# Dilated convolution with gated output on one core: order of the first and the last steps, and padded tiles at the end

## The chip, the core and the metric

The kernel runs on one core of one Trainium2 chip. The metric is the time of one launch in microseconds (us) on the device. A lower time is better. A core has five engines with instruction streams of their own: TensorE (PE in the profile, with its weight loads as PEld), VectorE (DVE), ScalarE (ACT), GpSimd (POOL) and SyncE (SP). DMA transfers are issued by SP, ACT and POOL and run beside the engines.

## The reference

The input x has two sequences of 16000 tokens with 144 channels. A causal convolution with 15 taps, two tokens apart, makes 288 channels. The first 144 go through tanh, the other 144 through a sigmoid, their product z goes through a 144 by 144 matrix. All arrays are bf16.

```python
B, T, D, K = (2, 16000, 144, 15)
def reference(x, w, w_o):
    dil = 2
    pad = (K - 1) * dil
    xp = jnp.pad(x, ((0, 0), (pad, 0), (0, 0)))
    h = jnp.einsum('btc,cd->btd', xp[:, pad:pad + T, :], w[0])
    for i in range(1, K):
        off = pad - i * dil
        h = h + jnp.einsum('btc,cd->btd', xp[:, off:off + T, :], w[i])
    f = h[..., :D]
    g = h[..., D:]
    z = jnp.tanh(f) * _sigmoid(g)
    return z @ w_o
```

## The kernel before

**Tiling.** The two sequences stand one behind the other with a gap of 32 zero tokens and are cut into ten blocks of 3072 tokens and one of 1536. A partition of an output tile stands for 48 tokens of one parity. A *unit* is half of a big block (`r` is 0 or 1), 128 partitions with 12 positions (`NCL`) each; the last block is one unit by itself (`r` is None). So there are 21 units, run in order by `unit(ui)`.

**The convolution.** Instead of 15 products per position the kernel forms sums and differences of x on DVE (`derive`: tiles S, D, E and those with 2, 4 and 42 behind the name) and sums and differences of the weights once at the start (H, G, GN, PW, WN and Wr). TensorE multiplies them, ACT and DVE combine the results (`take`, `add`, `A2_take`) into y. The 144 input channels are cut into 128, in tile xn, and the other 16. Those 16 are first *gathered* from x into a compact array rs in DRAM (`gather_r`, rows of 32 bytes), from which a transposing DMA loads tile rx (`load_r`), so that one partition group holds 16 channels of eight neighbouring tokens. From rx come Sr, Dr and Er, whose products with Wr end each accumulation.

**The start.** Before the weights are there, TensorE multiplies zeros from tile wz (`zeros_mm`, L298). Then it adds weights by products with the identity (`sum_pair`, `sum_one`, L293 with ident); ACT moves the sums into H and PW (L305, L310, L348). ACT also negates some weights: GN (L320), PW (L321), and, at L842 after the first products of block 0, `WN[:, 4:7]` from taps 12 to 14. ACT's queue issues two of the four weight loads and both gathers of block 0 (L124), SP's queue the other loads: xn of block 0, wr_f (the weights of the 16 channels), rx of block 0, then the gather and both loads of block 1. POOL zeroes the edges of rs, then clears wo_ab and the ends of the z tiles, then runs a one-element copy that reads rx of block 0 (L335), and only then issues the sixteen loads of the output weights wo_ab.

**The output.** z of a unit is one row of 12 x 144 = 1728 values per partition in one of two tiles zs of 1792 columns. A DMA transposes it in 128-column blocks into zT, and the products of `outproj` take two neighbouring blocks for each position (wo_ab holds the output weights at eight shifts, with zeros around). Results go to tile os and from there by `store` to DRAM.

**The end.** The last unit is finished in `end_unit`, in an order written out by hand. Here c is the last unit, pv the one before, p2 the one before that. z of the last unit is not transposed by DMA but by TensorE, in four groups (`end_T`): A and B hold four blocks of 128 columns each, C one block and then the first blocks of columns 0 to 287, D the blocks of columns 288 to 575. Since 288 is 128 + 128 + 32, the last block of C and of D is 32 columns wide. `end_cp` copies a group from PSUM to tile zeA, zeB, zeC or zeD with DVE, the narrow block by a second copy of 32 partitions. `end_mm` then makes one position from two blocks, the second with only m = 16 + o rows:

```python
mm(ps, [(cur["ze", t0][:, b0, :], wo_ab[:, o // 16, :]), (cur["ze", t1][0:m, b1, :], wo_ab[0:m, 8 + o // 16, :])], True)
```

PSUM is held as two x banks (each two banks of 512 columns wide, `x_bank`), three y banks (`y_bank`) and one o bank. The pool frees them in turn, so an operation that takes a bank waits for the one that last read it. `out_pv` takes six positions of pv into an x bank, `out_3` up to three of c into half an x bank or the o bank. The stores name their queues: those of pv go over POOL, of c positions 4 to 11 over SP three times and ACT once, and positions 0 to 3 over ACT three times and SP once. K_ keeps the instructions of each engine in the program's order.

Of the kernel before, what the change touches and what calls it, by code (L numbers as in the profile page):

```python
# [15 lines left out]
def kernel(  # L16
# [24 lines left out]
    nc = tc.nc  # L41
# [20 lines left out]
    def K_(ins):  # L62
        return tc.keep_in_program_order(ins)
# [127 lines left out]
    def tt(out_, a, b, op):  # L191
        return K_(nc.vector.tensor_tensor(out=out_, in0=a, in1=b, op=op))  # L192
# [91 lines left out]
    def x_bank():  # L284
        return ps_x.tile([P, 2, 512], F32, name="px")

    def y_bank():
        return ps_y.tile([P, 512], F32, name="py")

    def mm(ps, jobs, start, stop=True):  # L290
        n = len(jobs)
        for k, (l, r) in enumerate(jobs):
            K_(nc.tensor.matmul(ps, lhsT=l, rhs=r, start=start and k == 0, stop=stop and k == n - 1,  # L293
                                skip_group_check=not start))

    def zeros_mm(ps, n):
        for _ in range(n):
            K_(nc.tensor.matmul(ps, lhsT=wz[:, 0:P], rhs=wz[:], start=True, stop=True))  # L298
# [12 lines left out]

    for _ in range(2):
        ps = x_bank()
        zeros_mm(ps[:, 0, :], 3)
        zeros_mm(ps[:, 1, :], 3)
    for _ in range(3):
        zeros_mm(y_bank()[:], 1)
    K_(nc.vector.tensor_scalar(out=WN[:, 0:4, :], in0=w_all[:, 4:8, :], scalar1=-1.0, scalar2=None, op0=ALU.mult))
    for m in range(2):
        K_(nc.scalar.mul(out=GN[:, m, 3, :], in_=w_all[:, 7, :], mul=-1.0))  # L320
    K_(nc.scalar.mul(out=PW[:, 4:6, :], in_=w_all[:, 2:4, :], mul=-1.0))  # L321
    for e in range(2):
        gather_r(0, nc.scalar, (e, 1))
    load_r(0)
# [5 lines left out]
    wo_ab = const.tile([P, 16, D], BF16)  # L330
    K_(nc.gpsimd.memset(wo_ab[:], 0.0))
    zs = [const.tile([P, ZW], BF16, name=f"z{i}") for i in range(2)]
    for z_ in zs:
        K_(nc.gpsimd.memset(z_[:, NCL * D:ZW], 0.0))
    K_(nc.gpsimd.tensor_copy(out=warm[:], in_=blocks[0]["rx"][:, 1, RW[0] - 1:RW[0]]))  # L335
    for j in range(8):
        o = 16 * j
# [110 lines left out]
    def take_o(cur, c0, n, po, eng):  # L448
        dst = cur["os"][:, c0:c0 + n, :].rearrange("p a d -> p (a d)")
        if eng is nc.scalar:  # L450
            K_(nc.scalar.copy(out=dst, in_=po[:, 0:n * D]))  # L451
        else:
            K_(nc.vector.tensor_copy(out=dst, in_=po[:, 0:n * D]))

    def store(cur, c0=0, c1=NCL, engs=None):
        engs = engs or [nc.sync]
        k = 0
        bi = cur["blk"]["bi"]
        npd = BTOK[bi] // 48
        segs_ = store_segs(bi)  # L460
        if c1 <= 4:
            segs_ = [(p0, n + 1, ncl, b, tk) for (p0, n, ncl, b, tk) in segs_ if ncl == NCL]
        for (p0, n, ncl, b, tk) in segs_:
            if ncl <= c0:
                continue
            nc_ = min(ncl, c1) - c0
            for r in ((0, 1) if cur["r"] is None else (cur["r"],)):
                for e in range(2):
                    dst = bass.AP(out.tensor, out[b, tk + 4 * c0 + 2 * r + e, 0].offset,
                                  [[48 * D, n], [4 * D, nc_], [1, D]])  # L470
                    s = npd * e + p0 + (2 * npd * r if cur["r"] is None else 0)
                    K_(engs[k % len(engs)].dma_start(out=dst, in_=cur["os"][s:s + n, c0:c0 + nc_, :]))
                    k += 1


    ZE = {"A": [(4 * D + k * P, P) for k in range(4)], "B": [(4 * D + k * P, P) for k in range(4, 8)],
          "C": [(4 * D + 8 * P, P), (0, P), (P, P), (2 * P, 2 * D - 2 * P)],
          "D": [(2 * D, P), (2 * D + P, P), (2 * D + 2 * P, 2 * D - 2 * P)]}

    def end_T(cur, nm, ps):  # L480
        z = zs[cur["id"] % 2]
        ps = ps[:].bitcast(BF16)
        for k, (o, wd) in enumerate(ZE[nm]):
            K_(nc.tensor.transpose(ps[0:wd, k * P:(k + 1) * P], z[:, o:o + wd], ident[:]))  # L484
        return ps

    def end_cp(cur, nm, ps, eng):
        n = len(ZE[nm])
        sb = cur["ze", nm] = g_pool.tile([P, 4, P], BF16, name="ze" + nm)
        wd = ZE[nm][-1][1]  # L490
        m = n if wd == P else n - 1
        cp = K_scalar if eng is nc.scalar else K_vector
        cp(sb[:, 0:m].rearrange("p k s -> p (k s)"), ps[:, 0:m * P])
        if m < n:
            cp(sb[0:wd, m], ps[0:wd, m * P:n * P])

    def K_scalar(o, i):
        K_(nc.scalar.copy(out=o, in_=i))

    def K_vector(o, i):  # L500
        K_(nc.vector.tensor_copy(out=o, in_=i))

    def end_mm(cur, ps, j):

        blk, o = divmod(D * (j - 4 if j >= 4 else j % 2), P)
        m = CR + o
        at_ = lambda b: (("ABC"[b // 4], b % 4) if j >= 4 else ("CD"[j // 2], b + 1 - j // 2))
        (t0, b0), (t1, b1) = at_(blk), at_(blk + 1)
        mm(ps, [(cur["ze", t0][:, b0, :], wo_ab[:, o // 16, :]), (cur["ze", t1][0:m, b1, :], wo_ab[0:m, 8 + o // 16, :])], True)


    units = [(bi, r) for bi in range(NBIG) for r in range(2)] + [(NBIG, None)]
# [100 lines left out]
    def end_unit(c, pv, p2):  # L613
        V, A = nc.vector, nc.scalar
        c["os"] = os_pool.tile([P, NCL, D], BF16, name="os")

        def evict(cur, c0, n, ps, eng):

            dst = cur["os"][:, c0:c0 + 2 * n, :].rearrange("p (b a) d -> p b (a d)", b=2)
            if eng is A:  # L620
                K_(A.copy(out=dst, in_=ps[:, :, 0:n * D]))
            else:
                K_(V.tensor_copy(out=dst, in_=ps[:, :, 0:n * D]))  # L623

        def out_pv(c0, eng):
            ps = x_bank()
            for k in range(6):
                blk, o = divmod(D * (c0 + k), P)
                mm(ps[:, k // 3, (k % 3) * D:(k % 3 + 1) * D],
                   [(pv["zT"][:, blk, :], wo_ab[:, o // 16, :]), (pv["zT"][:, blk + 1, :], wo_ab[:, 8 + o // 16, :])], True)  # L630
            evict(pv, c0, 3, ps, eng)

        def out_3(cls, ps):
            for k, j in enumerate(cls):
                end_mm(c, ps[:, k * D:(k + 1) * D], j)

        def gate_half(h, k):
            if h == k == 0:
                c["g", 0] = [g_pool.tile([P, 4, D], BF16, name=nm) for nm in ("th", "sg")] + [4]
            K_(A.activation(out=c["g", 0][k][:, 2 * h:2 * h + 2], in_=c["y"][:, 2 * h:2 * h + 2, D * k:D * k + D],  # L640
                            func=(ACT.Tanh, ACT.Sigmoid)[k]))

        def mul_half(h):
            th, sg = (t[:, 2 * h:2 * h + 2].rearrange("p a d -> p (a d)") for t in c["g", 0][:2])
            tt(zs[c["id"] % 2][:, 2 * h * D:(2 * h + 2) * D], th, sg, ALU.mult)

        pe_A(c, c["Y", 3, 0][:, 0:D2], 3, 0, 0)
        take(c, 3, 0, 0)
        gate_act(c, 4, 1)
        outproj(p2, 3, V)  # L650
        store(p2)
        pe_A(c, c["Y", 3, 1][:, 0:D2], 3, 0, 1)
        take(c, 3, 0, 1)
        gate_mul(c, 4)
        gate_act(c, 8, 0)
        gate_act(c, 8, 1)
        for b1 in range(2):
            pe_A(c, c["X", 3][:, b1, 0:D2], 3, 1, b1)
        tA = end_T(c, "A", y_bank())
        gate_half(0, 0)  # L660
        gate_half(0, 1)
        take(c, 3, 1)
        gate_half(1, 0)
        gate_half(1, 1)
        gate_mul(c, 8)
        mul_half(0)
        end_cp(c, "A", tA, V)
        out_pv(0, A)
        store(pv, 0, 6, [nc.gpsimd])
        tB = end_T(c, "B", y_bank())  # L670
        tC = end_T(c, "C", y_bank())
        mul_half(1)
        end_cp(c, "B", tB, V)
        end_cp(c, "C", tC, V)
        x4 = x_bank()
        out_3((4, 5, 6), x4[:, 0])
        tD = end_T(c, "D", y_bank())
        out_pv(6, A)
        store(pv, 6, 12, [nc.gpsimd])
        out_3((7, 8, 9), x4[:, 1])  # L680
        end_cp(c, "D", tD, V)
        po = ps_o.tile([P, 512], F32, name="po")
        out_3((10, 11), po)
        evict(c, 4, 3, x4, V)
        take_o(c, 10, 2, po, A)
        store(c, 4, 12, [nc.sync, nc.sync, nc.sync, nc.scalar])
        x0 = x_bank()
        out_3((0, 1), x0[:, 0])
        out_3((2, 3), x0[:, 1])
        evict(c, 0, 2, x0, A)  # L690
        store(c, 0, 4, [nc.scalar, nc.sync, nc.scalar, nc.scalar])

    sums = []
    LAST = {4: lambda: gather_r(NBIG, nc.sync), 6: lambda: last_x(0), 8: lambda: last_x(1),
# [144 lines left out]
    pe_A(c, c["X", 1][:, 0, 0:D2], 1, 1, 0, "main")  # L839
    nxt()  # L840
    pe_A(c, c["Y", 1, 0][:, 0:D2], 1, 0, 0, "main")
    K_(nc.scalar.mul(out=WN[:, 4:7, :], in_=w_all[:, 12:15, :], mul=-1.0))  # L842
    for nm in ("E", "Sr", "Dr", "E2", "E4"):
        derive(0, nm)
    for ui in range(NU):
# [31 lines left out]
```

## Time and profile before

| | |
|---|---|
| median of 3 runs | 319.1 us (319.06, 319.10, 320.29) |
| profiled execution | 318.24 us, of which the span from first to last instruction is 316.4 us |
| PE busy | 305.3 us (96%), 2651 matmuls |
| PEld, DVE, ACT busy | 289.3 us (91%), 276.4 us (87%), 267.1 us (84%) |
| POOL busy | 24.4 us (8%) |
| DMA | 39.70 MB, mean 125 GB/s |
| chain that ended last | PE 91%, ACT 5%, DVE 2% |
| mean granted TensorE clock | 0.991 |

"Busy" is the time in which an engine has at least one instruction running; matmuls overlap, so their length (0.226 us for 128 x 144) is more than the distance between their starts. The chain is followed back from the last instruction, at each step to what released it. In a timeline a row is a run of like instructions: its start, its length, the engine, the line of the program, the tiles written and read, the count, and in brackets the engine's idle time before it and who ended it. "ACTq", "SPq" and "POOL" rows with DMA are the issuing of transfers; their landing is seen in the semaphores. A span of one execution stands below the device time of that execution by 1.8 us here.

### The profile page before, as it was taken

How to read it: one execution, taken by the hardware profiler on the slowest of the kernel's cores; microseconds unless marked ns; L12 is line 12 of the kernel's file. 1: busy time of each engine (PE TensorE's matmuls, PEld its weight loads, DVE VectorE, ACT ScalarE, POOL GpSimd, SP SyncE). 2: the span in 40 equal slices, each digit the busy share in tenths (PEclk: the TensorE clock that was granted, in tenths of full speed). 3: DMA queues.
4: the chain of work that ended last, by engine and by line, in shares of the span. 5: the costliest groups of instructions: out<-in, count | busy, mean ns of one | idle time of the engine just before them, and what ended most of it. 6: DMA issues, size and time to landing. Idle time of an engine off the chain costs nothing.

```text
span 316.4 us, 6932 instructions
## 1 busy us (share of the span) xinstructions
PE 305.3 (96%) x2651; PEld 289.3 (91%) x2651; DVE 276.4 (87%) x486; ACT 267.1 (84%) x629; POOL 24.4 (8%) x51
## 2 busy tenths in 40 slices
PE   8889999999999999999999999999999999999991
PEld 3678999999999999999999999999999999999870
DVE  3898999899899989989998998999899889869770
ACT  3667978989898898988989898898988989898870
POOL 8773000000000000000000000000000000000011
PEclk9999999999999999999999999999999999999996
DMA  8997194796959886795975947878395954724343
GB/s 210 141 151 128 37 139 61 156 130 99 178 101 140 111 181 121 112 201 121 143 143 125 173 86 147 167 113 178 67 181 96 167 111 88 147 58 92 60 85 77
DMA packets 176361, 39.70 MB, mean 125 GB/s; under 512 B 173640, under 2 KB 176168, under 8 KB 176328
## 3 DMA queue, kind: packets, MB, share of 16 engines
q1 hardware_dynamic: 170444, 37.70, 67.5%
q0 software_dynamic: 1248, 0.79, 1.5%
q10 hardware_dynamic: 4635, 0.77, 1.4%
q8 instruction: 20, 0.33, 0.4%
q14 instruction: 14, 0.11, 0.1%
HBM read 3.70 MB, written 11.44 MB: 48 GB/s over the span
## 4 chain that ended last, share of the span: by engine, by line
PE 91%; ACT 5%; DVE 2%; issue 1%; ACTq 0%
PE px L293 51%; PE py L293 28%; PE po L293 9%; PE px L298 2%; DVE y L192 1%; ACT py L522 1%; ACT th L420 1%; ACT m L544 1%; ACT px L522 0%; ACT sg L420 0%; PE py L484 0%; DVE os L623 0%; ACT H L310 0%; ACT WN L842 0%; PE py L298 0%
## 5 line engine op out<-in xcount | busy, mean ns | idle before, releaser
L293 PEld LDWEIGHTS <-E 128*128 128x128 bf16 x798 | 99.8, 142 | 2.4 <-issue 1.4
L522 ACT COPY py<-px 128x288 f32<-128x288 f32 x126 | 45.6, 388 | 26.0 <-PE px L293 15.6
L293 PEld LDWEIGHTS <-D 128*128 128x128 bf16 x462 | 58.5, 138 | 2.9 <-issue 0.7
L293 PEld LDWEIGHTS <-S 128*128 128x128 bf16 x462 | 56.1, 138 | 2.8 <-issue 1.6
L293 PE MATMUL px<-H,E 128*128 128x288 bf16 x252 | 44.7, 286 | 0.8 <-ACT m L544 0.5
L420 ACT ACTIVATE th<-y 128x576 bf16<-128x576 bf16 x62 | 42.5, 686 | 0.8 <-DVE y L192 0.8
L522 ACT COPY px<-px 128x288 f32<-128x288 f32 x105 | 42.3, 403 | 0.5 <-PE px L293 0.5
L420 ACT ACTIVATE sg<-y 128x576 bf16<-128x576 bf16 x62 | 41.8, 674 | 0.0
L192 DVE TENSOR_TENSOR z<-th,sg 128x576 bf16<-128x576 bf16 (+1 forms) x64 | 28.7, 450 | 14.2 <-ACT sg L420 14.1
L293 PE MATMUL po<-wo_ab,zT 128*128 128x144 bf16 x456 | 40.9, 226 | 0.0
L451 ACT CAST os<-po 128x432 bf16<-128x432 f32 x76 | 39.4, 519 | 0.0
L544 ACT ACTIVATE m<-py 128x288 bf16<-128x288 f32 x84 | 35.3, 420 | 2.9
L293 PEld LDWEIGHTS <-zT 128*128 128x128 bf16 x480 | 35.4, 98 | 2.0
L293 PE MATMUL px<-w_all,E 128*128 128x288 bf16 x210 | 35.2, 286 | 0.0
L192 DVE TENSOR_TENSOR E<-E 128x1280 bf16<-128x1280 bf16 (+4 forms) x33 | 33.8, 1053 | 0.4
L293 PE MATMUL py<-WN,E 128*128 128x288 bf16 x168 | 30.1, 286 | 0.0
L544 ACT ACTIVATE m<-px 128x576 bf16<-128x576 f32 x42 | 27.3, 650 | 1.2 <-PE px L293 0.2
L293 PE MATMUL px<-G,S 128*128 128x288 bf16 x168 | 27.5, 286 | 0.6 <-ACT py L522 0.6
L293 PE MATMUL py<-GN,S 128*128 128x288 bf16 x168 | 27.4, 286 | 0.0
L293 PE MATMUL py<-GN,D 128*128 128x288 bf16 x168 | 27.4, 286 | 0.0
L293 PE MATMUL px<-G,D 128*128 128x288 bf16 x168 | 26.6, 286 | 0.0
L293 PEld LDWEIGHTS <-Er 128*128 128x128 bf16 x168 | 23.9, 143 | 0.2
(96 smaller groups left out, 532.6 us busy)
## 6 DMA issues: line engine op xcount, KB each, us to landing
out_dram<-os SPq DMA_DIRECT2D x34, 216.0 KB
rs<-in_x_dram SPq DMA_DIRECT2D x8, 97.0 KB
out_dram<-os SPq DMA_DIRECT2D x4, 168.8 KB
w_all<-in_w_dram SPq DMA_DIRECT2D x2, 288.0 KB
xnl<-in_x_dram SPq DMA_DIRECT2D x2, 270.0 KB
rxl<-rs SPq DMA_DIRECT2D x2, 256.0 KB
out_dram<-os POOLq DMA_DIRECT2D x4, 108.0 KB, 2.8
xn<-in_x_dram SPq DMA_TRANSPOSE x22
```

What stands on the lines that cost most here:

```text
L192: return K_(nc.vector.tensor_tensor(out=out_, in0=a, in1=b, op=op))
L293: K_(nc.tensor.matmul(ps, lhsT=l, rhs=r, start=start and k == 0, stop=stop and k == n - 1, skip_group_check=not start))
L298: K_(nc.tensor.matmul(ps, lhsT=wz[:, 0:P], rhs=wz[:], start=True, stop=True))
L420: K_(nc.scalar.activation(out=cur["g", c0][k][:, 0:n], in_=cur["y"][:, c0:c0 + n, D * k:D * k + D], func=(ACT.Tanh, ACT.Sigmoid)[k]))
L451: K_(nc.scalar.copy(out=dst, in_=po[:, 0:n * D]))
L522: K_(nc.scalar.copy(out=dst, in_=src))
L544: K_(nc.scalar.activation(out=dst, in_=ps, func=ACT.Copy, scale=0.5))
```

## The change

At the start:
- `zeros_mm` runs twice and once instead of three and three times for each of two x banks, so six fewer products of zeros.
- The negation into `WN[:, 4:7]` moves on ACT from L842 to behind the other negations, ahead of the two gathers of block 0, which ACT's queue issues.

At the end:
- Columns 0 to 575 of z of the last unit are written to two tiles of their own, zh, 384 columns each, of which POOL clears the last 96 at the start. All transposes, copies and products at the end now have 128 columns and rows. `end_cp` is one DVE copy for each group.
- Both halves of pv's output are multiplied and evicted before the transposes B and C. The first half is stored by SP instead of POOL.
- Positions 4 to 6 go to the o bank and 7 to 9 and 10 to 11 to y banks, instead of an x bank and the o bank. DVE evicts 4 to 6 and 7 to 9 apart (432 columns each), in place of one eviction of 864.
- The stores of the last unit come behind its last eviction, and name their queues anew: SP, ACT, POOL, SP and ACT, SP, ACT, SP.

```diff
         ps = x_bank()
-        zeros_mm(ps[:, 0, :], 3)
-        zeros_mm(ps[:, 1, :], 3)
+        zeros_mm(ps[:, 0, :], 2)
+        zeros_mm(ps[:, 1, :], 1)
...
     K_(nc.scalar.mul(out=PW[:, 4:6, :], in_=w_all[:, 2:4, :], mul=-1.0))
+    K_(nc.scalar.mul(out=WN[:, 4:7, :], in_=w_all[:, 12:15, :], mul=-1.0))
     for e in range(2):
         gather_r(0, nc.scalar, (e, 1))
     load_r(0)
...
+    zh = [const.tile([P, 3 * P], BF16, name=f"zh{i}") for i in range(2)]
...
+    for z_ in zh:
+        K_(nc.gpsimd.memset(z_[:, 2 * D:3 * P], 0.0))
...
-          "C": [(4 * D + 8 * P, P), (0, P), (P, P), (2 * P, 2 * D - 2 * P)],
-          "D": [(2 * D, P), (2 * D + P, P), (2 * D + 2 * P, 2 * D - 2 * P)]}
+          "C": [z_end[:, 4 * D + 8 * P:4 * D + 9 * P]] + [zh[0][:, k * P:(k + 1) * P] for k in range(3)],
+          "D": [zh[1][:, k * P:(k + 1) * P] for k in range(3)]}
...
-            K_(nc.tensor.transpose(ps[0:wd, k * P:(k + 1) * P], z[:, o:o + wd], ident[:]))
+            K_(nc.tensor.transpose(ps[:, k * P:(k + 1) * P], blk, ident[:]))
...
+        K_(nc.vector.tensor_copy(out=sb[:].rearrange("p k s -> p (k s)")[:, 0:n], in_=ps[:, 0:n]))
...
-        mm(ps, [(cur["ze", t0][:, b0, :], wo_ab[:, o // 16, :]), (cur["ze", t1][0:m, b1, :], wo_ab[0:m, 8 + o // 16, :])], True)
+        mm(ps, [(cur["ze", t0][:, b0, :], wo_ab[:, o // 16, :]), (cur["ze", t1][:, b1, :], wo_ab[:, 8 + o // 16, :])], True)
...
-            tt(zs[c["id"] % 2][:, 2 * h * D:(2 * h + 2) * D], th, sg, ALU.mult)
+            tt(zh[h][:, 0:2 * D], th, sg, ALU.mult)
...
         out_pv(0, A)
-        store(pv, 0, 6, [nc.gpsimd])
-        tB = end_T(c, "B", y_bank())
-        tC = end_T(c, "C", y_bank())
-        mul_half(1)
-        end_cp(c, "B", tB, V)
-        end_cp(c, "C", tC, V)
-        x4 = x_bank()
-        out_3((4, 5, 6), x4[:, 0])
-        tD = end_T(c, "D", y_bank())
+        store(pv, 0, 6)
         out_pv(6, A)
         store(pv, 6, 12, [nc.gpsimd])
-        out_3((7, 8, 9), x4[:, 1])
-        end_cp(c, "D", tD, V)
-        po = ps_o.tile([P, 512], F32, name="po")
-        out_3((10, 11), po)
-        evict(c, 4, 3, x4, V)
-        take_o(c, 10, 2, po, A)
-        store(c, 4, 12, [nc.sync, nc.sync, nc.sync, nc.scalar])
+        tB = end_T("B", y_bank())
+        tC = end_T("C", y_bank())
+        mul_half(1)
+        end_cp(c, "B", tB)
+        p4 = ps_o.tile([P, 512], F32, name="po")
+        out_3((4, 5, 6), p4)
+        tD = end_T("D", y_bank())
+        end_cp(c, "C", tC)
+        end_cp(c, "D", tD)
+        p7 = y_bank()
+        out_3((7, 8, 9), p7)
+        take_o(c, 4, 3, p4, V)
+        p10 = y_bank()
+        out_3((10, 11), p10)
+        take_o(c, 10, 2, p10, A)
+        take_o(c, 7, 3, p7, V)
         x0 = x_bank()
         out_3((0, 1), x0[:, 0])
         out_3((2, 3), x0[:, 1])
         evict(c, 0, 2, x0, A)
-        store(c, 0, 4, [nc.scalar, nc.sync, nc.scalar, nc.scalar])
+        store(c, 4, 12, [nc.sync, nc.scalar, nc.gpsimd, nc.sync])
+        store(c, 0, 4, [nc.scalar, nc.sync, nc.scalar, nc.sync])
...
-    K_(nc.scalar.mul(out=WN[:, 4:7, :], in_=w_all[:, 12:15, :], mul=-1.0))
     for nm in ("E", "Sr", "Dr", "E2", "E4"):
         derive(0, nm)
```

More of the change, by code (lines that the diff above doesn't have):

```diff
@@ L473, in store, with end_T, end_cp @@
                     k += 1
-    ZE = {"A": [(4 * D + k * P, P) for k in range(4)], "B": [(4 * D + k * P, P) for k in range(4, 8)],
-          "C": [(4 * D + 8 * P, P), (0, P), (P, P), (2 * P, 2 * D - 2 * P)],
-          "D": [(2 * D, P), (2 * D + P, P), (2 * D + 2 * P, 2 * D - 2 * P)]}
-    def end_T(cur, nm, ps):
-        z = zs[cur["id"] % 2]
+    z_end = zs[(2 * NBIG) % 2]
+    ZE = {"A": [z_end[:, 4 * D + k * P:4 * D + (k + 1) * P] for k in range(4)],
+          "B": [z_end[:, 4 * D + k * P:4 * D + (k + 1) * P] for k in range(4, 8)],
+          "C": [z_end[:, 4 * D + 8 * P:4 * D + 9 * P]] + [zh[0][:, k * P:(k + 1) * P] for k in range(3)],
+          "D": [zh[1][:, k * P:(k + 1) * P] for k in range(3)]}
+    def end_T(nm, ps):
         ps = ps[:].bitcast(BF16)
-        for k, (o, wd) in enumerate(ZE[nm]):
-            K_(nc.tensor.transpose(ps[0:wd, k * P:(k + 1) * P], z[:, o:o + wd], ident[:]))
-        return ps
-    def end_cp(cur, nm, ps, eng):
-        n = len(ZE[nm])
+        for k, blk in enumerate(ZE[nm]):
+            K_(nc.tensor.transpose(ps[:, k * P:(k + 1) * P], blk, ident[:]))
+        return ps
+    def end_cp(cur, nm, ps):
+        n = len(ZE[nm]) * P
         sb = cur["ze", nm] = g_pool.tile([P, 4, P], BF16, name="ze" + nm)
[L490 to L501, printed above, removed]
+        K_(nc.vector.tensor_copy(out=sb[:].rearrange("p k s -> p (k s)")[:, 0:n], in_=ps[:, 0:n]))
     def end_mm(cur, ps, j):
         blk, o = divmod(D * (j - 4 if j >= 4 else j % 2), P)
-        m = CR + o
         at_ = lambda b: (("ABC"[b // 4], b % 4) if j >= 4 else ("CD"[j // 2], b + 1 - j // 2))
         (t0, b0), (t1, b1) = at_(blk), at_(blk + 1)
-        mm(ps, [(cur["ze", t0][:, b0, :], wo_ab[:, o // 16, :]), (cur["ze", t1][0:m, b1, :], wo_ab[0:m, 8 + o // 16, :])], True)
+        mm(ps, [(cur["ze", t0][:, b0, :], wo_ab[:, o // 16, :]), (cur["ze", t1][:, b1, :], wo_ab[:, 8 + o // 16, :])], True)
     units = [(bi, r) for bi in range(NBIG) for r in range(2)] + [(NBIG, None)]
@@ L658, in end_unit @@
             pe_A(c, c["X", 3][:, b1, 0:D2], 3, 1, b1)
-        tA = end_T(c, "A", y_bank())
+        tA = end_T("A", y_bank())
         gate_half(0, 0)
@@ L666, in end_unit @@
         mul_half(0)
-        end_cp(c, "A", tA, V)
+        end_cp(c, "A", tA)
         out_pv(0, A)
-        store(pv, 0, 6, [nc.gpsimd])
-        tB = end_T(c, "B", y_bank())
-        tC = end_T(c, "C", y_bank())
-        mul_half(1)
-        end_cp(c, "B", tB, V)
-        end_cp(c, "C", tC, V)
-        x4 = x_bank()
-        out_3((4, 5, 6), x4[:, 0])
-        tD = end_T(c, "D", y_bank())
+        store(pv, 0, 6)
         out_pv(6, A)
         store(pv, 6, 12, [nc.gpsimd])
-        out_3((7, 8, 9), x4[:, 1])
-        end_cp(c, "D", tD, V)
-        po = ps_o.tile([P, 512], F32, name="po")
-        out_3((10, 11), po)
-        evict(c, 4, 3, x4, V)
-        take_o(c, 10, 2, po, A)
-        store(c, 4, 12, [nc.sync, nc.sync, nc.sync, nc.scalar])
+        tB = end_T("B", y_bank())
[14 more added lines that the diff above has]
+        take_o(c, 7, 3, p7, V)
         x0 = x_bank()
```

## The prediction

> **What bounds the kernel now.** I read the page first: PE is busy 96% of the span and 91% of the chain that ended last is PE. So the middle (about 32 us to 300 us) is a full PE stream that this change does not touch. Two stretches are left in which something else can be late: the start and the last 16 us. I read both in the timeline, then the chain, the windows, and single records of matmuls and semaphores.
>
> The end, in the timeline (start, length, engine, line, tiles):
>
> ```profile
> 303.12 0.91 PE L293 MATMUL px<-wo_ab,zT 128*128 128x144 bf16 x12
> 304.28 0.72 PE L484 MATMUL py<-ident,z 128*128 128x128 bf16 x8 [0.24 <-DVE z L192]
> 304.94 1.07 PE L293 MATMUL px<-wo_ab,zeA 128*128 128x144 bf16 x6
> 308.21 0.72 PE L293 MATMUL px<-wo_ab,zeC 128*128 128x144 bf16 x4
> 308.86 0.73 PE L293 MATMUL px<-wo_ab,zeD 128*128 128x144 bf16 x4
> 309.69 0.64 ACT L621 CAST os<-px 128x576 bf16<-128x576 f32 x1 [1.17 <-PE px L293]
> 310.36 1.70 ACTq L472 DMA_DIRECT2D out_dram<-os  x3
> ```
>
> Twelve full products take 0.91 us: a matmul lasts 0.226, so they start 0.063 apart. Six on zeA take 1.07, 0.167 apart. In the records every second one has 16, 32 or 48 rows of weights. The chain then runs PE, the last eviction on ACT, and three stores issued one after another on ACT's queue until 312.06. By the semaphore records the last store lands at 314.40; 2.0 us of waits and drains follow to 316.4.
>
> The windows (length, busy PE, PEld, DVE, ACT, POOL, granted clock, DMA share, GB/s):
>
> ```profile
> 4.00:8.00 4.00, 4.00 (x17) 1.79 (x16) 1.82 (x4) 1.65 (x5) 3.58 (x8) 1.00 1.24 292
> 8.00:10.00 2.00, 2.00 (x19) 1.56 (x17) 1.93 (x4) 0.65 (x1) 2.00 (x5) 1.00 1.44 150
> 310.00:312.00 2.00, 0.00 (x0) 0.00 (x0) 0.00 (x0) 0.33 (x1) 0.00 (x0) 0.62 0.85 174
> ```
>
> The DMA engines are full from 4 to 10 us and again, at 0.85, while the last stores drain.
>
> The start, in the timeline:
>
> ```profile
> 1.19 5.30 PE L298 MATMUL px<-wz 128*128 128x512 bf16 x12 [1.19 <-DVE wz L116]
> 5.00 0.62 ACTq L124 DMA_DIRECT2D rs<-in_x_dram  x1
> 7.14 3.51 PE L293 MATMUL px<-w_all,ident 128*128 128x288 bf16 x27
> 11.40 1.23 DVE L192 TENSOR_TENSOR S<-xn 128x2048 bf16<-128x2048 bf16 x1 [1.48 <-DMA xn<-in_x_dram]
> 19.68 0.68 DVE L192 TENSOR_TENSOR Sr<-rx 128x1024 bf16<-128x1024 bf16 x1
> 20.27 0.92 ACT L842 ACTIVATE WN<-w_all 128x864 bf16<-128x864 bf16 x1
> ```
>
> DVE waits 1.48 us for the second half of xn (landed 11.28) and then works almost without a gap until Er ends at 25.24. So the start is set by when xn lands, with an ACT and PE chain nearly as late beside it, in which WN stands.
>
> **Part by part: the start.** Six of the fifteen products of zeros go. They start 0.427 us apart, so the nine that are left end at 1.19 + 9 x 0.427 = 5.03, just after the first weights (w_all) land at 4.97, and the ident sums start there instead of at 7.14. The records show the pitch of 512 columns halve to 0.21 only after 6.7 us, so about seven sums run at 0.24 apiece instead of 0.12. PE is then (7.14 + 7 x 0.1225) - 6.7 = 1.3 us ahead. Alone this gives almost nothing, because S waits for xn; it removes the ACT backlog (PW evicted until 13.57, delaying the px copy to 13.47) that would be next late, some 0.3 us.
>
> The Trainium skill ("TensorE: Matmul & The Clock Gate", Part 1) says that the array runs at half clock until about 3.4 us of sustained activity, whatever the matmuls are. By that rule the sums warm the array as zeros do, unless a gap opens before them; the pitch agrees with a change of rate, at 5.5 us after the first matmul, and the granted clock column (1.00 there) does not show it.
>
> WN moves ahead of block 0's gather on ACT. WN waits for w_all's taps 12 to 14, which land at 6.87, so the gather is issued at about 6.93 instead of 5.00: +1.9 us. Its 32-byte packets flow from 8.0 to 10.8 in the trace, 3.0 us behind the issue; now from about 9.9. About 1195 of 3072 packets (10.7 ns each) ran before 9.2, while xn's packets were still flowing: 1195 x 10.7 / 16 = 0.8 us of DMA time returned to xn. xn's first half landed 1.2 us after its packets ended (about 7.2 to 8.42), the second 2.1 us after (9.2 to 11.28), behind the gather. With 8.6 + 1.2 it lands near 9.9 and S starts about 9.95 (DVE's earlier work ends at 9.93): up to 1.4 us sooner. The other bound is 0, if xn's landing does not move.
>
> What queues behind: SP's load of rx waits for the gather (first at 10.88, now about 12.2), so rx lands at about 18.4 instead of 17.13. Sr would be due at 19.68 - 1.4 = 18.3, so DVE waits about 0.1. Behind it on SP the block 1 loads slip by 1.3: xn of block 1 (landed 22.97, used at 32.29) and rx (27.48, used at 36.93) have over 9 us. POOL's warm copy waits for rx too and holds the wo_ab loads (landed 29.69, first used at 44.27). At the old place WN leaves ACT: the chain's 0.81 us becomes about 0.2, since m then waits for the Sr products ending at 20.89. Both chains move by 1.1 to 1.4. I take **1.1 us** for the start, bounds 0.2 (WN alone) and 1.4. The two zh memsets on POOL (0.17 us each for z) stand ahead of the same wait for rx: nothing.
>
> **Part by part: the end.** PE: each narrow product costs about 0.10 us on itself and again on the next, until full tiles follow. The records give 0.167 apart on zeA (six), 0.165 on zeC and zeD (eight), 0.16 twice around the 64-row zeB, and 0.15 to 0.20 around the two 32-column transposes. With padding: 6 x 0.104 + 8 x 0.10 + 0.2 + 2 x 0.2 = 2.0 us of PE. Products at 80 to 112 rows already run at 0.065, so their padding is free.
>
> The Trainium skill ("TensorEngine Tiling (Array Packing)", Tiling Modes, Key Properties) says that changing the tiling mode drains TensorE; the 0.167 against 0.063 agrees.
>
> Order: pv's second half (12 products) now fills the 0.24 us in which PE waited for z. Counting on from 303.91 (bank free after take at 303.87) with 0.0625 per product and 0.056 per transpose: pv until 304.66, tB and tC until 305.11, columns 4 to 6 until 305.49, tD until 305.66, 7 to 9 until 306.03, 10 and 11 until 306.28, 0 to 3 until 306.78, ended by 306.94 instead of 309.59. The waits added: 7 to 9 need zeB's bank (DVE copy done 305.52), 0 to 3 need zeD (306.24); both are met. DVE: zeB 305.10, zeC 0.42, zeD 0.35, then two evictions of 432 at 0.61 (row L453) in place of one of 864 at 1.06; done 307.28 instead of 308.93. ACT's last eviction ends at 307.63 instead of 310.33. So the stores of columns 4 to 11 start 1.65 us sooner, those of 0 to 3 2.7 us sooner, and spread as two SP, one ACT, one POOL and two and two they are issued by about 308.9 instead of 312.06.
>
> What is late next is the DMA engines. Packets of 288 bytes take 21.9 ns; the records show 9 of 16 engines complete for each 27-row store. Those nine have 3 x 24 + 32 packets, 2.3 us, plus POOL's share of 0.37 and some 0.55 left of pv's second half: from 308.5 to about 311.7. Landing follows the last packet by 0.94 as before (313.46 to 314.40): about 312.5. I take **2.0 us**; if the issues decided, it would be 3.1.
>
> The Trainium skill ("DMA: Bandwidth & Descriptors", Issuing engines are not separate DMA queues) says that issuing from several engines only saves issue time, since all share the 16 DMA engines; by that rule the gain stays near 2.0 and not 3.1, and the 0.85 share above agrees.
>
> **Sum.** 1.1 + 2.0 = 3.1 us. The profiled execution took 318.2 (span 316.4 and 1.8 around it), 0.9 below the median of 319.1; the same difference is kept: 319.1 - 3.1 = 316.0. About 0.5% (1.6 us) is what a measurement here can tell from no change.
>
> **Rivals.**
> - *xn does not land sooner.* The landing may be held by its own transposition and not by the gather. Then the start gives 0.2: 319.1 - 2.2 = 316.9. For: its packets ended at 9.2 with little gather ahead of them. Against: the first half needed only 1.2 us to land.
> - *Issue time decides the end.* 3.1 there: 319.1 - 4.2 = 314.9. For: three ACT stores in series close the trace. Against: DMA share 0.85.
> - *POOL ends last.* Its fourth store took 3.9 us to land, and its drain ended 4.8 after that issue. With a store issued until 308.4 its drain ends by 313.2 and the end gains 1.3: 316.7.
> - *The padding does not do what it says.* If products stay 0.167 apart for another reason (a bank, a port), only order and queues count, about 1.0 us at the end, and a start of 0.2: 317.9, no change.
> - *Slower: the gather holds Sr.* rx has 2.55 us of cover (17.13 to 19.68). If the gather behind wr_f's loads slips rx by more, DVE waits at Sr and every later step with it; beyond 2.55 + 2.0 the whole is slower, and at a slip of 6.5 us it is 321.1. Against: the expected slip is 1.3, and the whole gather took 6.75 us in full contention.
>
> **How the numbers follow.** Forecast 0.50; xn unmoved 0.17; issue decides 0.11; POOL last 0.10; padding idle 0.07; gather holds Sr 0.05. The first four are faster by over 1.6 us except their upper tails (0.05, which I put to no change); so faster 0.83, same 0.12, slower 0.05. The range: least gain of the two bounds that I still count, 0.2 + 1.2, gives 317.7; the largest, 1.1 + 3.1 and a little of the 1.4, gives 314.8.
>
> **What would show it.** Right: S starts near 10, Sr near 18.4, the ident sums at 5.0; in the end zeA, zeC and zeD groups of six and four in about 0.54 and 0.41, ACT's last eviction ending near 307.6 less the start's gain, the last landing 3 us sooner. Wrong: S still at 11.4, Sr waiting for rx by over 1 us, narrow pitch with full tiles, or a POOL drain that ends after SP's last wait.

## The result and the profile after

The changed kernel takes 316.25 us (median of six runs, 316.17 to 316.84), the kernel before 318.96 us in the same comparison (six runs, 318.65 to 320.29). The ratio of the two is 0.9914 with a 95% interval of 0.9895 to 0.9932, so 2.7 us less (2.2 to 3.3). The forecast was 316.0 us, 3.1 less.

The profiled execution took 316.84 us with a span of 315.0. It is the slowest of the six runs, while the one profiled before (318.24) is among the fastest of its kernel, so this pair shows a difference of only 1.4 us. The page after (span; busy time of PE; shares of the chain that ended last):

```profile
span 315.0 us, 6922 instructions
PE 301.7 (96%) x2645; PEld 288.1 (91%) x2645; DVE 276.2 (88%) x485; ACT 267.1 (85%) x629; POOL 23.4 (7%) x52
PE 87%; ACT 3%; DVE 3%; DMA 2%; SPq 1%; issue 1%; POOLq 0%; POOL 0%; DVEq 0%
```

PE is 3.6 us less busy (305.3 to 301.7). POOL is in the chain now, where it was not before. The start, in the timeline:

```profile
1.19 2.74 PE L298 MATMUL px<-wz 128*128 128x512 bf16 x6 [1.19 <-DVE wz L116]
5.14 3.50 PE L293 MATMUL px<-w_all,ident 128*128 128x288 bf16 x23
7.29 0.93 ACT L322 ACTIVATE WN<-w_all 128x864 bf16<-128x864 bf16 x1 [0.55 <-DMA w_all<-in_w_dram]
7.30 1.55 ACTq L124 DMA_DIRECT2D rs<-in_x_dram  x2
11.17 1.23 DVE L192 TENSOR_TENSOR S<-xn 128x2048 bf16<-128x2048 bf16 x1 [1.00 <-DMA xn<-in_x_dram]
```

The ident sums start at 5.14 instead of 7.14 (5.03 was worked out). The gather is issued at 7.30 instead of 5.00 (forecast 6.93, but taps 12 to 14 of w_all landed 0.4 us later than before, at 7.27). S starts at 11.17 and not near 10. The first weights were late by the same 0.4 us (5.37 instead of 4.97). This one trace does not tell whether xn really gained nothing.

The end, in the timeline. First the issuing of the last stores on POOL and SP in the kernel before:

```profile
308.45 1.32 POOL L472 DMA_DIRECT2D out_dram<-os  x2 [1.37 <-ACT os L621]
308.99 2.14 SPq L472 DMA_DIRECT2D out_dram<-os  x4
```

Then the changed kernel:

```profile
304.59 0.54 PE L293 MATMUL po<-wo_ab,zeA 128*128 128x144 bf16 x6
304.94 5.08 SPq L476 DMA_DIRECT2D out_dram<-os  x6
305.75 0.41 PE L293 MATMUL px<-wo_ab,zeC 128*128 128x144 bf16 x4
305.99 2.12 POOL L476 DMA_DIRECT2D out_dram<-os  x3 [204.59 <-ACT os L614]
306.01 0.41 PE L293 MATMUL px<-wo_ab,zeD 128*128 128x144 bf16 x4
306.46 0.64 ACT L614 CAST os<-px 128x576 bf16<-128x576 f32 x1
306.80 2.03 ACTq L476 DMA_DIRECT2D out_dram<-os  x3
```

With padded tiles the six products on zeA take 0.54 us (1.07 before), the four on zeC and on zeD 0.41 each (0.72 and 0.73). ACT's last eviction ends at 307.10 instead of 310.33. Counted from the end of the last convolution products (those on `c["X", 3]`, called X3 here; ended at 303.06 before, 302.55 after) it comes at 4.5 us instead of 7.3. Yet the span ends only 12.5 us after that point instead of 13.4. The windows of the last microseconds show why (length, busy PE, PEld, DVE, ACT, POOL, clock, DMA share, GB/s):

```profile
308.00:310.00 2.00, 0.00 (x0) 0.00 (x0) 0.00 (x0) 0.00 (x0) 0.11 (x1) 1.00 0.80 155
310.00:312.00 2.00, 0.00 (x0) 0.00 (x0) 0.00 (x0) 0.00 (x0) 0.00 (x0) 0.51 0.47 96
```

Past 307.10 no engine computes any more. POOL (until 308.11), ACT and SP only issue stores. By the records of the single issues, the issue of SP's last store ended at 310.02, and the store landed at 312.90. Each engine's records end with a *drain* instruction and a few short ones. SP's drain stood behind its waits for the landings and ended at 313.24. POOL's last store landed at 312.24, but POOL's drain, begun at 307.36, ended at 313.76, later than SP's. The last pieces of the chain lead into the stores of POOL (start, length, engine and line; lines left out are marked, and the last row, L866, is POOL's drain):

```profile
306.76 0.58 POOL out_dram L476
...
307.36 0.75 POOLq L866
```

### The profile page after: what moved, and what is told of

Read it like the earlier page. It is cut to its first block, busy times and chain, and to the rows that moved or that the text cites. A ratio compares the mean times of both kernels' runs of the same rounds, so it can differ in the third digit from the quotient of the medians.

```text
span 315.0 us, 6922 instructions
## 1 busy us (share of the span) xinstructions
PE 301.7 (96%) x2645; PEld 288.1 (91%) x2645; DVE 276.2 (88%) x485; ACT 267.1 (85%) x629; POOL 23.4 (7%) x52
## 4 chain that ended last, share of the span: by engine, by line
PE 87%; ACT 3%; DVE 3%; DMA 2%; SPq 1%; issue 1%; POOLq 0%; POOL 0%; DVEq 0%
PE px L293 49%; PE py L293 28%; PE po L293 9%; DMA xn<-in_x_dram 2%; SPq L143 1%; DVE y L192 1%; DVE S L192 1%; ACT th L424 1%; ACT m L537 1%; ACT py L515 1%; ACT sg L424 0%; DVE H L192 0%; DVE D L192 0%; SPq L261 0%; ACT px L515 0%
## 5 line engine op out<-in xcount | busy, mean ns | idle before, releaser
L192 DVE TENSOR_TENSOR z<-th,sg 128x576 bf16<-128x576 bf16 x62 | 28.1, 453 | 14.2 <-ACT sg L424 14.1
```

## The experiments

Each kernel was timed in five rounds beside the kernel before, whose medians were 318.72 us (start_only, end_only, pad_only, order_only), 318.68 (wn_only, zeros_only, no_pool_last, no_pool_narrow) and 318.53 (the other four). Where kernels of different groups are compared, the ratios to the kernel before count as well as the medians.

### The two halves of the change

**start_only**: both edits of the start, with the end as before.

```diff
-        zeros_mm(ps[:, 0, :], 3)
-        zeros_mm(ps[:, 1, :], 3)
+        zeros_mm(ps[:, 0, :], 2)
+        zeros_mm(ps[:, 1, :], 1)
...
+    K_(nc.scalar.mul(out=WN[:, 4:7, :], in_=w_all[:, 12:15, :], mul=-1.0))
     for e in range(2):
         gather_r(0, nc.scalar, (e, 1))
...
-    K_(nc.scalar.mul(out=WN[:, 4:7, :], in_=w_all[:, 12:15, :], mul=-1.0))
```

> Both edits of the start, the end as before. Theory A (the prediction): the gather held xn's landing, so S starts near 10 instead of 11.4 and about 1.1 us is saved (318.0 less 1.1 from the median of before, about 0.35%). Theory B (read from the trace of after, where xn's second half still landed at 11.05 with no gather packet beside it): the landing is held by its own transposition, S moves by 0.6 at most, and 0.2 to 0.6 us is saved, by WN off the chain and the ACT backlog gone.

Measured: 316.80 us (316.56 to 317.23), ratio 0.993 (0.991 to 0.995). Its timeline:

```profile
7.06 1.52 ACTq L124 DMA_DIRECT2D rs<-in_x_dram  x2
10.44 1.23 DVE L192 TENSOR_TENSOR S<-xn 128x2048 bf16<-128x2048 bf16 x1 [0.40 <-DMA xn<-in_x_dram]
12.61 0.38 ACT L523 COPY px<-px 128x288 f32<-128x288 f32 x1
18.75 0.69 DVE L192 TENSOR_TENSOR Sr<-rx 128x1024 bf16<-128x1024 bf16 x1
```

S starts 0.96 us sooner than before (11.40), Sr 0.93, the S of block 1 1.08 (31.21 against 32.29). rx landed at 18.65, just before Sr. So xn does land sooner once the gather is out of its way: its second half lands at 10.32 here and between 9.89 and 10.58 in the five other kernels below that have this start, against 11.28 before. The changed kernel's own profile, with 11.05, is the one exception.

**end_only**: all edits of the end, with the start as before (the diff of the change without the lines above).

> All edits of the end, the start as before. Theory A: 2.0 us saved (0.63%), set by the DMA engines' backlog. Theory B (from the trace of after): the stores are issued up to 310.0, POOL's drain ends 1.5 us after its last store lands and later than SP's last wait, so only 0.9 to 1.5 us is saved.

Measured: 317.59 us (317.30 to 318.26), ratio 0.996 (0.9944 to 0.9976). So the end alone gives 1.1 us by the medians and 1.3 by the ratio, not the 2.0 of the prediction. The two halves give 1.9 and 1.1 us, 3.0 together, beside 2.7 for the whole change.

### The two parts of the start

**wn_only** has only the move of the negation, **zeros_only** only the six products of zeros less (each one half of the diff above).

> Only the negation into WN stands ahead of block 0's gather; all products of zeros and the end as before. Theory A (the late gather frees the DMA engines for xn): xn's second half lands near 10.4 instead of 11.3 to 11.7, S starts 0.8 to 1.2 us sooner, and 1.0 to 1.9 us is saved, nearly all that both start edits gave. Rival B (the products of zeros are what counts): under 0.5 us.

> Only six products of zeros fewer; WN, the gather and the end as before. Theory A: the ident sums start near 5.0, but S waits for xn at 11.3 or later as before, so 0 to 0.3 us is saved. Rival B: 1 us or more.

Measured: wn_only 317.62 us (316.66 to 318.10), ratio 0.9955 (0.9938 to 0.9972); zeros_only 318.52 us (317.92 to 319.72), ratio 0.9999 (0.9984 to 1.0014). The timeline of wn_only:

```profile
9.97 1.23 DVE L192 TENSOR_TENSOR S<-xn 128x2048 bf16<-128x2048 bf16 x1 [0.16 <-DMA xn<-in_x_dram]
13.62 0.41 ACT L523 COPY px<-px 128x288 f32<-128x288 f32 x1
```

and that of zeros_only:

```profile
5.00 4.16 PE L293 MATMUL px<-w_all,ident 128*128 128x288 bf16 x27
11.40 1.22 DVE L192 TENSOR_TENSOR S<-xn 128x2048 bf16<-128x2048 bf16 x1 [1.56 <-DMA xn<-in_x_dram]
```

With the zeros alone PE is 2 us ahead, and S still waits for xn at 11.40: nothing is gained. With WN alone S starts 1.43 us sooner, and 1.1 us is saved by the medians, where both edits save 1.9. The sums hold PE and ACT until the px copy at 13.62, a microsecond later than in start_only. Er ends 1.37 us sooner, while the S of block 1 starts only 0.32 sooner (31.97): the lead is used up in between. With both edits block 1 keeps 1.08. Each edit takes away the wait that would hide the other.

### The two parts of the end

**pad_only**: full tiles (zh, full transposes, copies and products), but order, banks and queues as before.

```diff
-            K_(nc.tensor.transpose(ps[0:wd, k * P:(k + 1) * P], z[:, o:o + wd], ident[:]))
+            K_(nc.tensor.transpose(ps[:, k * P:(k + 1) * P], blk, ident[:]))
...
-        mm(ps, [(cur["ze", t0][:, b0, :], wo_ab[:, o // 16, :]), (cur["ze", t1][0:m, b1, :], wo_ab[0:m, 8 + o // 16, :])], True)
+        mm(ps, [(cur["ze", t0][:, b0, :], wo_ab[:, o // 16, :]), (cur["ze", t1][:, b1, :], wo_ab[:, 8 + o // 16, :])], True)
```

**order_only**: order, banks and queues of the change, but narrow tiles as before (the products keep `0:m`, the last blocks of C and D stay 32 columns wide). The first piece is shown against the changed kernel, the second against the kernel before.

```diff
+            wd = ZW_[nm] if k == len(ZE[nm]) - 1 else P
+            K_(nc.tensor.transpose(ps[0:wd, k * P:(k + 1) * P], blk, ident[:]))
...
         out_pv(0, A)
-        store(pv, 0, 6, [nc.gpsimd])
+        store(pv, 0, 6)
         out_pv(6, A)
         store(pv, 6, 12, [nc.gpsimd])
```

> Full 128-column and 128-row tiles in the order, the banks and the queues of before. Theory A: the 2.0 us of PE reach the last eviction but for 0.2 us of waits (ACT's last eviction ends near 308.5 instead of 310.33), and 1.2 to 1.8 us reach the end. Rival: the stores' backlog hides PE's time there, and under 0.5 us is saved.

> The new order, banks and stores with the narrow tiles of before (32-column transposes, products with 16 to 112 rows). Theory A: PE keeps 2.0 us of narrow products, only the 0.24 us wait for z and the serial stores go, so 0.5 to 1.0 us is saved. Rival (padding is idle, order is all): as much as with both, 1.5 to 2 us, with the zeC and zeD products still 0.165 us apart.

Measured: pad_only 318.35 us (317.53 to 319.17), ratio 0.9973 (0.9956 to 0.9989); order_only 317.45 us (317.08 to 318.39), ratio 0.9956 (0.9938 to 0.9975), the same as end_only. So pad_only saves 0.4 us by the medians and 0.9 by the ratio, less than the 1.2 expected, and order_only 1.3 to 1.4, which is between its two expectations. Which of order, banks and queues gives it was not told apart. The timeline of order_only:

```profile
305.14 1.07 PE L293 MATMUL po<-wo_ab,zeA 128*128 128x144 bf16 x6
308.80 0.64 ACT L620 CAST os<-px 128x576 bf16<-128x576 f32 x1 [0.83 <-PE px L293]
```

In end_only the same eviction starts at 307.38, which is 3.9 us after the end of X3 (303.48) instead of 5.9 (302.90):

```profile
305.51 0.54 PE L293 MATMUL po<-wo_ab,zeA 128*128 128x144 bf16 x6
307.38 0.64 ACT L613 CAST os<-px 128x576 bf16<-128x576 f32 x1
```

From the end of X3 to the end of the span end_only takes 12.18 us, order_only 12.21, pad_only 13.14, the kernel before 13.39. The padding makes PE faster by what was worked out, and with the new order nothing of it reaches the end. The records of the issues show where it goes. In order_only no issue of SP or ACT takes over 0.63 us. In end_only ACT's last eviction ends 2.0 us nearer to X3, but the last three issues take 0.91 to 1.08 each, and the last one ends 7.30 us after X3, in order_only 7.43. Something behind the evictions decides.

### What decides instead: POOL's last store, and the backlog of stores

**no_pool_last**: the changed kernel, with the one store of the last unit that POOL issues given to ACT. **no_pool_narrow**: the same with the narrow tiles of order_only.

```diff
-        store(c, 4, 12, [nc.sync, nc.scalar, nc.gpsimd, nc.sync])
+        store(c, 4, 12, [nc.sync, nc.scalar, nc.scalar, nc.sync])
```

> The changed kernel with the one store of the last unit that POOL issued moved to ACT. Theory C (POOL's drain ends about 1.5 us after its last store lands and now ends last): the drain ends before SP's last wait, and 0.3 to 0.5 us is saved against the changed kernel (near 315.8). Rival D (the last landing decides and ACT's queue is longer): no gain, or 0.2 to 0.5 us slower.

> The same with the narrow tiles of before, so padding alone differs from the run before this. Theory C (the end is a backlog of stores, which hides PE's 2.0 us): within 0.4 us of it. Rival E (PE's time decides once POOL is out of the way): 1 us or more slower than it.

Measured: no_pool_last 315.30 us (314.86 to 315.82), ratio 0.989 (0.9871 to 0.9909); no_pool_narrow 315.46 us (314.95 to 315.63), ratio 0.9893 (0.9874 to 0.9911). All runs of no_pool_last lie below all those of the changed kernel, by 0.95 us in the median and by 0.8 in the ratios (0.989 and 0.9914), more than the 0.3 to 0.5 expected: it beats both kernels. Its timeline:

```profile
304.35 5.76 SPq L476 DMA_DIRECT2D out_dram<-os  x6
305.39 1.35 POOL L476 DMA_DIRECT2D out_dram<-os  x2 [204.67 <-ACT os L614]
305.86 0.64 ACT L614 CAST os<-px 128x576 bf16<-128x576 f32 x1
306.21 3.15 ACTq L476 DMA_DIRECT2D out_dram<-os  x4
```

POOL now stores only pv's second half. Its last store lands at 310.06 and its drain ends at 311.54, before SP's at 312.32. So the forecast's rival that POOL ends last was true of the change as made. The last landing comes 0.24 us nearer to X3 as well (10.11 after it instead of 10.35). Padding is again worth nothing (315.30 beside 315.46). SP's last store was not issued until 309.78: it waited 1.66 us for an earlier store of ACT, which signals by the same semaphore and landed at 309.77.

**pv_pool**: no_pool_last with pv's first half stored by POOL, as before the change.

```diff
         out_pv(0, A)
-        store(pv, 0, 6)
+        store(pv, 0, 6, [nc.gpsimd])
```

> The run without POOL's last store, with pv's first half stored by POOL again, so that POOL issues pv's four stores and SP and ACT only the last unit's eight. SP's last store waited for an earlier store on its semaphore until 309.8 there; with eight stores for eight semaphores no wait is left. If that wait counts: 0.3 to 0.7 us less than that run (near 314.8). If POOL's queue ends last again, or the engines' backlog decides: the same or up to 0.5 us more.

Measured: 316.00 us (315.42 to 316.07), ratio 0.9914 (0.9901 to 0.9927): no gain, rather a loss of 0.7 us against no_pool_last, with runs that overlap. Its timeline shows four stores in a row on POOL:

```profile
304.77 2.66 POOL L476 DMA_DIRECT2D out_dram<-os  x4 [203.85 <-ACT os L614]
```

They land until 311.51, POOL's drain ends at 313.08 and SP's at 312.95. POOL is last again, by a little. Here no store waits for another's semaphore, and still the last landing follows ACT's last eviction by 5.6 us, as in no_pool_last. So that wait by itself does not make the landing late.

**no_pv_store** and **no_pv_narrow**: no_pool_last and no_pool_narrow without any of pv's four stores. They leave that unit out of the output, and show what the end costs without the backlog that it makes.

```diff
         out_pv(0, A)
-        store(pv, 0, 6)
         out_pv(6, A)
-        store(pv, 6, 12, [nc.gpsimd])
```

> The run without POOL's last store, and none of pv's four stores: 1536 of the 2848 packets at the end are left out, so the output lacks that unit. Theory C (a backlog of packets decides the end): the last landing follows ACT's last eviction by 4 to 4.5 us instead of 5.6, so 1 to 1.5 us less than that run. Rival (issue and latency of the last unit's stores decide): under 0.4 us less.

> The same with the narrow tiles, and without pv's stores. Theory C: with the backlog gone padding's PE time shows, and this is 0.8 to 1.8 us slower than the run before it. Rival: the same within 0.3 us, so something else than pv's packets hides PE's time.

Measured: no_pv_store 313.95 us (313.92 to 314.05), ratio 0.9854 (0.9842 to 0.9867); no_pv_narrow 315.18 us (315.11 to 315.26), ratio 0.9892 (0.988 to 0.9905). Now the padding shows, with 1.23 us of the 2.0 by which ACT's last eviction moves. The timeline of no_pv_store:

```profile
305.59 0.64 ACT L614 CAST os<-px 128x576 bf16<-128x576 f32 x1
305.92 1.80 SPq L476 DMA_DIRECT2D out_dram<-os  x4
305.94 1.94 ACTq L476 DMA_DIRECT2D out_dram<-os  x4
```

and that of no_pv_narrow:

```profile
307.61 0.64 ACT L621 CAST os<-px 128x576 bf16<-128x576 f32 x1 [0.83 <-PE px L293]
```

In no_pv_store eight stores on two queues are issued from 305.92 to 307.89, and the last lands 4.0 us after ACT's last eviction ends (306.23 to 310.19). With pv's four stores ahead of them the last issue in no_pool_last ends at 310.10, and the landing follows the eviction by 5.6 us. The backlog of pv's stores thus costs 1.35 us by the medians (315.30 less 313.95) and 1.15 by the ratios, and as long as it stands it hides the padding. From first to last instruction the difference is larger, 1.85 us (median spans of 313.50 and 311.65): in the two kernels without pv's stores 2.3 us of the device time lie outside the span instead of 1.8, and no trace shows why.

### A gather later still

**late_gather**: the changed kernel, with the gather and the loads behind it (on SP and POOL) moved below ACT's copy into H, so that it leaves xn alone and presses on rx.

```diff
+    ps0 = x_bank()
...
+    K_(nc.scalar.copy(out=H[:, 0, 4:6, :], in_=ps0[:, :, 0:D2]))
     for e in range(2):
         gather_r(0, nc.scalar, (e, 1))
...
-    ps0 = x_bank()
...
-    K_(nc.scalar.copy(out=H[:, 0, 4:6, :], in_=ps0[:, :, 0:D2]))
```

> The changed kernel with block 0's gather, and all of SP's and POOL's work behind it, moved further down: ACT issues the gather behind its second eviction into H, near 9.5 instead of 7. Theory A (the gather's slip has a limit, where Sr waits for rx): S stays near 10.4, rx lands near 21 instead of 18.7, DVE waits 2 to 2.5 us at Sr, and the kernel is 1.5 to 2.5 us slower than the changed one (317.8 to 318.7). Rival (DVE's order has room behind Sr): under 0.5 us slower.

Measured: 318.49 us, but from 315.94 to 320.03; ratio 0.9985 (0.9957 to 1.0013). Its timeline:

```profile
7.72 0.63 ACTq L124 DMA_DIRECT2D rs<-in_x_dram  x1
10.06 1.23 DVE L192 TENSOR_TENSOR S<-xn 128x2048 bf16<-128x2048 bf16 x1
18.88 0.69 DVE L192 TENSOR_TENSOR Sr<-rx 128x1024 bf16<-128x1024 bf16 x1 [0.45 <-DMA rx<-rs]
```

The gather is issued at 7.72 and not near 9.5, while ACT's first copy into H (7.62 to 8.25) still runs and before the second starts (8.15). S starts at 10.06, and Sr waits 0.45 us for rx, which landed at 18.78: the cover of rx is used up, as the prediction put it, but far from the 2 to 2.5 us expected. The median is 2.2 us slower than the changed kernel, inside the 1.5 to 2.5 expected, but the trace does not show that this comes from Sr. Its execution has a span of 314.2 us, and the median span of the twelve is 316.7: five runs took 315.94 to 317.15 us, seven 318.31 to 320.03. That the gather holds Sr by more in those seven would fit, but no trace shows it. It stays open.

## Why the prediction was right, and where its sum was wrong

**The total**: 3.1 us forecast, 2.7 measured, by a split that was not the forecast one. The end gave less than its 2.0 us and the start, by the medians, more than its 1.1; that the two errors nearly cancel is luck.

**The start, 1.1 us**: the mechanism held. xn's second half lands at 10.3 in start_only and 9.9 in wn_only (9.9 forecast, 11.28 before). One reading on the way was off: the gather's packets began 1.65 us behind its issue in start_only (8.71 for 7.06) and not 3.0, yet only 158 of them ran before 9.2, against the 1195 counted before the change. In the profiles of kernels with this start, X3 ends 0.51 us sooner than before in the changed kernel, where w_all was late, and 0.95 to 1.37 in six others (late_gather left out), around the 1.1 forecast; in four other profiles without both edits of the start (end_only, pad_only, order_only, zeros_only) it ends between 302.90 and 303.48. The means, 301.96 and, with the kernel before, 303.13, are 1.2 us apart. That xn might not move fell as a rival. The medians give more, 1.9 us for start_only (interval 1.6 to 2.9). Most of the excess over the profiled pair is in the choice of the two executions: the span profiled before (316.4) is 0.4 us below the median span of its runs beside start_only (316.8), and that of start_only (315.4) is 0.4 above its own (315.0). That fewer zeros alone give "almost nothing" is shown. That their number decides how much of WN's gain lasts was worked out for the px copy only, at 0.3 us; by the S of block 1 it is 0.76 (1.08 less 0.32).

The Trainium skill ("TensorE: Matmul & The Clock Gate", Part 1) counts sustained activity, whatever the matmuls are. The trace agrees: with six fewer products of zeros the pitch of the sums still falls from 0.24 to 0.12 us at 6.2 us, which is 5.0 us after the first matmul. The time differs from the 3.4 us of that page: by the records of the granted clock in the fourteen profiles the full rate begins 2.9 (order_only) to 5.8 us (wn_only) after the first matmul. So the forecast's seven slow sums are those of one execution; in no_pool_last, with the same start, the sums are 0.12 us apart from the first one on.

**rx**: "DVE waits about 0.1" was close. rx landed at 18.65 in start_only, 0.1 us before Sr started at 18.75, so DVE did not wait. In the changed kernel it landed at 19.09, for an Sr at 19.44.

**The end, 2.0 us**: PE, DVE and ACT came as counted: groups of 0.54 and 0.41, and an ACT eviction that ends 2.73 us nearer to X3, forecast 2.7. The step that failed is what is late next. The landing was put at 312.5, which is 9.4 us after X3; it came at 10.35. The DMA term was thus too small by 0.9 us (by 0.7 in end_only and late_gather). The prediction let the stores be issued by 308.9 and counted only their packets, but the issues stretched: SP's last two took 0.98 and 1.19 us and ACT's last 0.97, where without pv's stores no issue took over 0.63. It takes the backlog of pv's stores and stores that come soon behind it: without pv's stores (no_pv_store) and with the later stores of order_only the issues did not stretch. How much of the lateness lies in the packets and how much in the issues was not told apart. On top of that POOL's drain ended 0.52 us behind SP's. That was a rival at 0.10, and it deserved more: POOL's last store landed 4.9 us after its issue began (307.38 to 312.24), a microsecond more than the 3.9 that the rival took. The measured 1.2 us (mean from X3's end to the span's end 13.48 in four profiles with the old end, 12.29 in three with the new) is close to the 1.3 of that rival, but its working was not: it put the drain's end 10.1 us after X3 (313.2 less 303.06), and the drain ended 11.2 after. Its 1.3 comes out if the 2.0 us of waits and drains of before still follow (316.4 less 313.2 less 2.0 is 1.2), and only 1.3 us followed (313.76 to 315.04). So here too two errors nearly cancel.

The rival that the issues decide had the end gain 3.1 us. It fell: the issues do come late, but as a loss. The Trainium skill ("DMA: Bandwidth & Descriptors", Issuing engines are not separate DMA queues) says that issue time "is usually small relative to the DMA itself", and that more issuers save only that. The second holds here (the gain did not reach 3.1). The first does not at this end: 0.9 to 1.2 us of issue stand beside 2.9 us from the end of the last issue to its landing (310.02 to 312.90).

**Padding idle**: the rival said that the products would stay 0.167 us apart. They did not, so it fell as stated, but its consequence was true for another reason: order, banks and queues alone give the whole gain of the end, since the backlog of stores hides the 2.0 us of PE.

**The gather holds Sr**: not in the changed kernel; in late_gather it begins to.

## What to carry to other kernels

At the end of a kernel count the stores as a queue of their own: their issues can stretch when others are in flight (0.63 to 1.19 us here), so PE time saved there is worth only what reaches the last landing. Keep the last stores off POOL if its drain could outlast that of the other queues. Two edits that each free one of two waits on the same step should be judged together, because either alone may show little.

## What the runs showed of the hardware

- POOL's drain ended 1.48 to 1.57 us after the landing of its last store in all twelve profiles whose end has a store on POOL; SP's ended 0.26 to 0.86 us after the last landing of all.
- The issue of a store on SP or ACT takes 0.31 to 0.63 us with little in flight (no_pv_store) and up to 1.19 us when it comes soon behind a backlog (the changed kernel).
- The queue of ACT issues a DMA while an earlier instruction of ACT still runs: in the changed kernel the gather at 7.30 us beside WN from 7.29 to 8.22.
